# A fused attention and two expert layers on one core: the first pair of heads loaded head by head on two queues, products of zeros meanwhile, the last sums finished one by one, tiles at multiples of 512 bytes

## The chip, the cores and the metric

The kernel runs on one core of a Trainium2 chip. The metric is the device time of one execution in microseconds (us), as the median of several runs. The engines are named as the profile names them: PE is TensorE's matmul and PEld its weight load, DVE is VectorE, ACT is ScalarE, POOL is GpSimd, and SP is SyncE, which here only issues DMAs. DMAs bring data from the chip's memory (HBM) into the on-chip memory SBUF; products are summed in PSUM.

## The reference

Four batches, 12 heads, 448 tokens, heads of 64. Attention with a soft cap on the scores, then two dense layers over 1792 tokens of width 768:

```
scores = cap * tanh((q @ k.T) / sqrt(64) / cap)
attn   = softmax(scores) @ v                       # 4 x 12 x 448 x 64
x      = attn as 1792 x 768
h      = x @ w_in           # 768 -> 2048
x      = (h * cos(h)) @ w_out                      # 2048 -> 768
a, b   = x @ w1, x @ w2     # 768 -> 1024
out    = ((a * b) @ w3) @ w_out2                   # 1024 -> 1024 -> 768
```

Everything is float32. The kernel folds the last two matrices into one, w34 = w3 @ w_out2, while the attention runs.

## The kernel before, in words

**Products.** Every dense product is made in three matmuls on pairs of "high" and "low" halves (`mm3`, lines 356 to 359): high times high, high times low, low times high, in the type float32r, 448 columns wide (384 for w34). The scores (lines 574 and 575) take two such matmuls on 112 columns of weights. The product of the probabilities with v (line 595) is plain float32, which the profile shows as two records for each product. There are 4,800 float32r matmuls (4,416 with 448 columns and 384 with 384) and 192 of plain float32.

**Attention.** A pair of heads is loaded at a time: `a_load` (line 488) brings q and k of one pair, each by two DMAs of 64 partitions x 2 x 448, because both halves of the partitions hold the same rows. `a_split` (line 502) makes from them `ks` (k's high part above, its low part below), `qh` and `ql` with two casts and two subtractions over both heads (896 columns). `c_S` makes the scores of 2 x 112 keys, `c_exp` applies tanh and exp on ACT in place and into `p`, `c_PV` multiplies with v. `c_consts` (line 555) sets the ones beside v on POOL. Before that, line 443 loads the cap by an SP DMA, lines 445 to 449 make its constants on DVE, and line 452 runs one tanh on a single column, so that ACT's table is loaded.

**Dense layers.** `make_w34` reads w3 and w_out2 (`raw` tiles), and its products lie between those of the attention. `moe1` runs over pairs of slices of 128 of the 2048 columns, and `moe2` over eight slices `fc` of the 1024. In `moe2`, `ab_unit` (line 1053) makes a * b for a slice: 36 matmuls on PE, then a copy on ACT, and a product, a cast and a subtraction on DVE, which leave `abh` and `abl`. `o_unit` (line 1069) multiplies one slice with w34 and adds it into six sums `acc[m]` in PSUM, m being one of six blocks of 128 output columns. One slice's `o_unit` stands behind the next slice's `ab_unit`. At the last slice each finished sum is copied into one of three `ob` tiles on ACT and written out by an SP DMA (lines 1084 and 1085).

**What sets the order.** Every operation is put into a `Plan` with a due time and the engines that may do it. `schedule` (line 169) plays the plan with assumed costs, in order of due times, once, when the program is built; the result is one fixed order for each engine. `at(g)` (line 476) gives the due time of step g of the attention; its numbers are in `PAR`. A `Ring` is a set of equal tiles that items take in turn; an item waits for a free tile. All DMAs stand in SP's row (`dma`, line 352). A DMA uses one of eight semaphores in turn, and the ninth waits for the first.

**Where tiles lie.** A tile is laid into SBUF when it is first used, behind the one before it, at the next multiple of 32 bytes of a partition. The small constants of 4 bytes come first, so that in the built program the first large tile `xh0` begins at byte 1312, which is 2 x 512 + 288. In the same way all tiles that a matmul reads begin 32, 64, 224, 288, 320 or 480 bytes behind a multiple of 512; weight slices are 512 bytes wide, and slices of 448 columns are 1792 bytes, which is 3.5 x 512.

Of the kernel before, what the change touches and what calls it, by code (L numbers as in the profile page):

```python
# [33 lines left out]
CAP_MAX = 40.0  # L34
TWOPI = 6.283185
# [34 lines left out]
class Ring:  # L70
    def __init__(self, plan, pool, tag, shape, dtype, n):
        self.pool, self.tag, self.shape, self.dtype = pool, tag, list(shape), dtype
        self.tiles, self.queue = {}, []
        self.free = [(0.0, k) for k in range(n)]
        plan.rings.append(self)
        pool.rings.append(self)

# [14 lines left out]
class Pool:  # L92
# [20 lines left out]
class Plan:  # L113
# [157 lines left out]
    p1=3.4, p2=6.2, gsw=48, t0=10.0,  # L271
# [8 lines left out]
    nq=1, nqh=2, nph=2, npl=2,  # L280
# [3 lines left out]
    p1=1.98, p2=2.86, gsw=90, t0=14.13, ql=10, qs=4, hsw=26, wb=(30.36, 107.61), we=(108.65, 207.54),  # L284
    m0=222.0, ua=13, pa=19.15, pu=14.2, nt=9, nph=3,
# [22 lines left out]
def program(  # L308
# [43 lines left out]
    def dma(due, dst, src, r=(), w=(), kb=115, write=False):  # L352
        plan.op(due, [("SP", 0.66, lambda: SP.dma_start(dst(), src()))], r=r, w=w,  # L353
                kb=kb)
# [17 lines left out]
    for name, kw in dict(const={}, xring={}, dram=dict(space=DRAM), psum=dict(space=PSUM), attn={}, lp={},  # L372
# [30 lines left out]
    def swap(*names, opens=()):  # L403


        def f():
            for n in names:
                pools[n].close()
            for n in opens:
                pools[n].open()  # L410

        plan.event(f, [pools[n] for n in names], [pools[n] for n in opens])

    for n in ("const", "xring", "dram", "psum", "attn", "wi", "wp"):
        pools[n].open()
    psum = pools["psum"].pool
# [26 lines left out]
    SP.dma_start(capt, cap.rearrange("(o n) -> o n", o=1).to_broadcast([P, 1]))  # L443
    pac = const([P, 1], "pac")
    DVE.tensor_scalar(nac, capt, -1.0, None, op0=ALU.mult)
# [6 lines left out]
    ACT.activation(warm, warm, AF.Tanh)  # L452
# [23 lines left out]
    def at(g):  # L476

        return G["t0"] + min(g, G["gsw"]) * G["p1"] + max(g - G["gsw"], 0) * G["p2"]
# [9 lines left out]
    def a_load(i, g):  # L488
        b, h = divmod(i, H)
        qk[i] = A["qr"].new(), A["kr"].new()  # L490
        for it, src in zip(qk[i], (q2, k2)):
            for j in range(2):
                r = it.at(j, rows(j))
                dma(at(g) if i else -99.0, r, lambda src=src: src[b, h // 2].rearrange("(i d) s -> d i s", i=2),
                    w=[r], kb=230)

# [64 lines left out]
    def cv_load(i, g):  # L561
# [3 lines left out]
        dma(at(g), vt[i][:, :, j, :], lambda: v[b, h], w=[vt[i]])  # L565
# [62 lines left out]
    def columns():  # L628
        c_consts()
        a_load(0, -2)  # L630
        a_split(0, -1)
# [400 lines left out]
    def moe2():  # L1032
        raw_r, x_r = ring("lp", "rawl", [P, 2 * DM], U32, 2), ring("lp", "xl_", [P, DM], F32, 2)
        a_r, ob_r = ring("qp", "a32", [P, S], F32, 2), ring("qp", "ob", [P, S], F32, 3)
# [34 lines left out]
        def o_unit(n, b, fc, due):  # L1069
            abh, abl = ab.pop((b, fc))  # L1070
# [92 lines left out]
```

## Time and profile before

| | |
|---|---|
| median of three runs | 1143.48 us (1141.04 to 1144.9) |
| the profiled execution's own time | 1141.23 us |
| its span, first to last instruction | 1139.2 us |
| PE busy | 1112.9 us, 98% of the span |
| DVE, ACT, POOL busy | 65%, 40%, 12% |
| DMA | 140.10 MB, 123 GB/s on the mean |

A run's own time is 2.0 us longer than the span of its instructions. A busy share of PE is not a rate: matmuls overlap, and a matmul's recorded length is about twice the distance to the next one. The distance from the start of one matmul to the start of the next says how fast PE goes. In the timeline a row gives the start, the length, the engine, the line, what is written from what, the number of merged instructions, and in brackets the idle time of the engine before it and what ended it. An engine's name with a q is its queue, which issues DMAs.

### The profile page before, as it was taken

To read this page: it belongs to the slowest core of one execution; us is meant where nothing else is said; L and a number is where in the kernel's file an instruction comes from. 1 tells how busy PE (TensorE), PEld (TensorE's weight loads), DVE (VectorE), ACT (ScalarE), POOL (GpSimd) and SP (SyncE) were. 2 spreads that over 40 slices of the span, in tenths; PEclk is the share of its full clock that TensorE was granted. 3 is DMA by queue.
4 is the path that set the end of the run, shared out by engine and by line. 5 is a ranking of instruction groups with operands and counts; after the bars stand their busy time and mean duration, and the time that the engine had idled before them with its cause. 6 is when DMAs were issued, how large, how long until landed. Compare 5 with 4: busy or idle time off the path is not lost.

```text
span 1139.2 us, 13718 instructions
## 1 busy us (share of the span) xinstructions
PE 1112.9 (98%) x5184; PEld 966.5 (85%) x5184; DVE 740.5 (65%) x1111; ACT 454.2 (40%) x581; POOL 133.3 (12%) x130
## 2 busy tenths in 40 slices
PE   5999999999999999999999999999999999999997
PEld 3777777778888888889999999998999999999996
DVE  5888777899998897787899877768831311311111
ACT  4887767877566655722454211113211101101001
POOL 2312111123231110110121000001200000000000
PEclk9999999999999999999999999999999999999999
DMA  8885765878756554337745211101401101101001
GB/s 231 229 224 149 212 185 171 231 210 252 209 154 188 190 148 158 130 100 235 272 127 180 70 56 56 29 1 69 140 15 41 57 1 41 57 1 40 10 1 51
DMA packets 83165, 140.10 MB, mean 123 GB/s; under 512 B 35986, under 2 KB 63634, under 8 KB 83090
## 3 DMA queue, kind: packets, MB, share of 16 engines
q1 hardware_dynamic: 83090, 139.14, 40.7%
q8 instruction: 42, 0.69, 0.2%
q14 instruction: 33, 0.27, 0.1%
HBM read 109.45 MB, written 29.58 MB: 122 GB/s over the span
## 4 chain that ended last, share of the span: by engine, by line
PE 93%; DVE 2%; DMA 1%; ACT 1%; SPq 1%; issue 0%; POOL 0%; ACTq 0%; DVEq 0%
PE bank L357 13%; PE bank L358 13%; PE bank L359 13%; PE double L358 12%; PE double L359 12%; PE double L357 12%; PE bank L595 12%; PE double L574 3%; PE double L575 3%; DMA rawc<-in_w_out 1%; SPq L353 1%; DMA kr<-in_k 0%; DVE w L343 0%; ACT double L584 0%; ACT p L584 0%
## 5 line engine op out<-in xcount | busy, mean ns | idle before, releaser
L343 DVE TENSOR_TENSOR a<-double,a 128x448 f32<-128x448 f32 x32 | 20.0, 625 | 240.1 <-PE double L359 237.7
L595 PE MATMUL bank<-p,v 112*128 112x448 f32 x384 | 161.3, 543 | 0.5 <-issue 0.5
L359 PE MATMUL double<-xh,w12l 128*128 128x448 f32 x378 | 137.8, 365 | 0.0
L358 PE MATMUL double<-xl,w12h 128*128 128x448 f32 x378 | 137.8, 365 | 0.0
L357 PE MATMUL double<-xh,w12h 128*128 128x448 f32 x378 | 137.4, 363 | 0.0
L584 ACT ACTIVATE double<-double,ts 112x896 f32<-112x896 f32 x96 | 94.1, 981 | 79.1 <-PE double L575 78.9
L333 ACT COPY a<-double 128x448 f32<-128x448 f32 x31 | 16.5, 533 | 254.1 <-PE double L359 254.1
L357 PE MATMUL bank<-xh,wih 128*128 128x448 f32 x270 | 107.9, 399 | 0.0
L595 PEld LDWEIGHTS bank<-p,v 112*128 112x128 f32 x384 | 72.6, 190 | 41.2 <-issue 38.3
L357 PE MATMUL bank<-gh,woh 128*128 128x448 f32 x260 | 102.1, 393 | 0.3 <-ACT hs L333 0.3
L358 PE MATMUL bank<-xl,wih 128*128 128x448 f32 x270 | 98.3, 364 | 0.0
L359 PE MATMUL bank<-xh,wil 128*128 128x448 f32 x270 | 98.0, 363 | 0.0
L584 ACT ACTIVATE p<-double,pac 112x896 f32<-112x896 f32 x96 | 96.7, 1010 | 2.0
L358 PE MATMUL bank<-gl,woh 128*128 128x448 f32 x260 | 95.2, 366 | 0.0
L359 PE MATMUL bank<-gh,wol 128*128 128x448 f32 x260 | 94.8, 365 | 0.0
L574 PE MATMUL double<-qh,ks 128*112 128x448 f32 x192 | 73.7, 384 | 14.4 <-DVE ks L343 10.3
L343 DVE TENSOR_TENSOR y<-bank,y 128x448 f32<-128x448 f32 x111 | 68.6, 619 | 23.0 <-PE bank L359 22.2
L358 PEld LDWEIGHTS double<-xl,w12h 128*128 128x128 f32 x378 | 71.0, 188 | 5.8
L357 PEld LDWEIGHTS double<-xh,w12h 128*128 128x128 f32 x378 | 70.8, 187 | 5.6
L359 PEld LDWEIGHTS double<-xh,w12l 128*128 128x128 f32 x378 | 71.0, 188 | 5.0
L575 PE MATMUL double<-ql,ks 128*112 128x448 f32 x192 | 72.1, 375 | 0.0
L357 PEld LDWEIGHTS bank<-xh,wih 128*128 128x128 f32 x270 | 50.8, 188 | 9.0 <-issue 5.0
(153 smaller groups left out, 2359.2 us busy)
## 6 DMA issues: line engine op xcount, KB each, us to landing
rawc<-in_w_out SPq DMA_DIRECT2D x16, 768.0 KB, 5.6
rawl<-in_w SPq DMA_DIRECT2D x16, 768.0 KB, 4.4
qr<-in_q SPq DMA_DIRECT2D x48, 224.0 KB, 4.6
kr<-in_k SPq DMA_DIRECT2D x48, 224.0 KB, 4.9
rawc<-in_w_in SPq DMA_DIRECT2D x13, 768.0 KB, 5.0
raw<-in_w3T SPq DMA_DIRECT2D x16, 512.0 KB, 5.8
raw<-in_w_out SPq DMA_DIRECT2D x8, 768.0 KB, 7.2
wo_d<-wx SPq DMA_DIRECT2D x16, 384.0 KB, 4.4
```

What stands on the lines that cost most here:

```text
L333: "A": ("ACT", (0.051 if psum else 0.094) + n / 1200, lambda: ACT.copy(dst(), src())),
L343: "D": ("DVE", 0.068 + n / 960, lambda: DVE.tensor_tensor(dst(), a(), b(), op=op))
L353: plan.op(due, [("SP", 0.66, lambda: SP.dma_start(dst(), src()))], r=r, w=w, kb=kb)
L357: PE.matmul(out, wh, xh, start=first, stop=False)
L358: PE.matmul(out, wh, xl, start=False, stop=False)
L359: PE.matmul(out, wl, xh, start=False, stop=last)
L574: PE.matmul(o, w, qh(), start=True, stop=False)
L575: PE.matmul(o, w, ql(), start=False, stop=True)
L584: lambda f=f, x=x, o=o: ACT.activation(o(), s(), f, scale=x[:CP]))],
L595: PE.matmul(pv()[:, :S], w()[:, 2 * c + n].rearrange("p a d -> p (a d)"), p()[:, n, :], start=c == 0 and n == 0, stop=c == NT - 1 and n == 1)
```

## The change

**The first pair of heads.** `a_first` takes the place of `a_load` and `a_split` for heads 0 and 1. Each head of q and k comes by DMAs of its own (64 partitions x 448, two for q and two for k); k is issued by SP and q by ACT. Its casts and subtractions are made for each head apart: k's cast on ACT, the rest on DVE. The v of head 0 is issued by ACT too, that of head 1 comes right behind the second pair. The second pair of heads is due before everything else that SP loads, and q and k have two tiles each instead of one (`nq`). The cap's DMA moves from SP to POOL. The tanh that loads ACT's table is now an operation of the plan, behind ACT's first DMAs. The due times of the first ten steps have a step of their own (`p0`, `g0`, `t0`).

**Products of zeros.** A tile of zeros is written by DVE first of all, and PE makes nine plain float32 products of 128 x 128 from it into a bank that nothing reads.

**The last sums.** The last slice but one has no `o_unit` of its own; the last `o_unit` goes over the six sums and adds both slices to each. `ob` has four tiles, and a write may go out on SP's or ACT's queue.

**Places in SBUF.** Two pads (224 bytes below, 480 above) and `settle` lay all tiles of a pool when it opens, those whose size is a multiple of 512 first. In the built program `xh0` begins at byte 2048, and every tile that a matmul of this program reads begins at a multiple of 512 or 256 bytes behind one.

```
+LINE = 512
+    def settle(self):
+        rings = sorted(self.rings, key=lambda r: r.bytes() % LINE > 0)
+        for r in rings:
+            for k in range(r.n):
+                r.tile(k)
...
-    p1=3.4, p2=6.2, gsw=48, t0=10.0,
+    p0=2.4, p1=3.4, p2=6.2, g0=10, gsw=48, t0=6.5,
...
-    nq=1, nqh=2, nph=2, npl=2,
+    nq=2, nqh=2, nph=2, npl=2,
...
+    def dma(due, dst, src, r=(), w=(), kb=115, write=False, on="S"):
+        opts = {
+            "S": ("SP", 0.66, lambda: SP.dma_start(dst(), src())),
+            "A": ("ACT", 0.66, lambda: ACT.dma_start(dst(), src())),
+        }
+        plan.op(due, [opts[e] for e in on], r=r, w=w, kb=kb)
...
+        pools["const"].pool.tile([P, 56], F32, name="pad", bufs=1)
+        pools["top"].pool.tile([P, 120], F32, name="pad2", bufs=1)
...
-    SP.dma_start(capt, cap.rearrange("(o n) -> o n", o=1).to_broadcast([P, 1]))
+    (SP if general else POOL).dma_start(capt, cap.rearrange("(o n) -> o n", o=1).to_broadcast([P, 1]))
...
+        z = const([P, P], "zeros")
+        DVE.memset(z, 0.0)
+        for _ in range(9):
+            PE.matmul(banks[7][:, :P], z, z, start=True, stop=True)
...
-    ACT.activation(warm, warm, AF.Tanh)
+    plan.op(-80.0, [("ACT", 1.4, lambda: ACT.activation(warm, warm, AF.Tanh))], w=[Ref(warm_i)])
...
-                dma(at(g) if i else -99.0, r, lambda src=src: src[b, h // 2].rearrange("(i d) s -> d i s", i=2),
+                dma(at(g) if i > 2 or general else -97.0, r, lambda src=src: src[b, h // 2].rearrange("(i d) s -> d i s", i=2),
...
+    def a_first():
+        q, k = qk[0] = A["qr"].new(), A["kr"].new()
+        qh, ql, ks = (A[x].new() for x in ("qh", "ql", "ks"))
+        for n in range(2):
+            for it, src, e in ((k, k2, "S"), (q, q2, "A")):
+                for j in range(2):
+                    r = it.at((n, j), lambda t, n=n, j=j: t[j * D:(j + 1) * D, n])
+                    dma(-99.0 + n, r, lambda src=src, n=n: src[0, 0, n * D:(n + 1) * D], w=[r], on=e)
...
+            plan.op(due, [("ACT", 0.47, lambda n=n, o=ks_: ACT.copy(o(), k.tile()[:, n]))], r=kj, w=[ks_])
+            low = ks.at(n, lower)
+            plan.op(due, [("DVE", 0.54, lambda n=n, o=low: DVE.tensor_tensor(
+                o(), k.tile()[D:, n], o().bitcast(F32), op=ALU.subtract), True)], r=[kj[1], low], w=[low])
+            plan.op(due - 0.5, [("DVE", 0.3, lambda n=n, o=qh_: DVE.tensor_copy(o(), q.tile()[:, n]), True)], r=qj, w=[qh_])
+            plan.op(due, [("DVE", 0.54, lambda n=n, o=ql_, h=qh_: DVE.tensor_tensor(
+                o(), q.tile()[:, n], h().bitcast(F32), op=ALU.subtract), True)], r=[*qj, qh_], w=[ql_])
...
-        dma(at(g), vt[i][:, :, j, :], lambda: v[b, h], w=[vt[i]])
+        dma(at(g) if i > 1 else -60.0, vt[i][:, :, j, :], lambda: v[b, h], w=[vt[i]], on="S" if i else "A")
...
+            for m in range(KD):
+                for fc, abh, abl, wh, wl in fcs:
...
+                if prev and (n, fc) != (B - 1, NF2 - 1):
+                    o_unit(prev[0], prev[1], prev[2:], due)
                     due += 3.4
-                prev = (n, b, fc)
+                    prev = []
+                prev = prev + [fc] if prev else [n, b, fc]
```

SP's row at the start of the program, before. `capt` is the cap, `qr` and `kr` are q and k of a pair, `raw` the words of w3 and w_out2:

```order
L443 DMA capt<-in_cap 128x1
L353 DMA qr_111<-in_q 64x2x448 x2
L353 DMA kr_114<-in_k 64x2x448 x2
L353 DMA raw_117<-in_w3T 128x1024
L353 DMA raw_119<-in_w_out 128x1536
L353 DMA raw_121<-in_w_out 128x1536
L353 DMA v_103<-in_v 112x4x64
```

The same place now:

```order
L366 DMA kr_132<-in_k 64x448 x4
L366 DMA qr_131<-in_q 64x2x448 x2
L366 DMA kr_133<-in_k 64x2x448 x2
L366 DMA v_122<-in_v 112x4x64
L366 DMA raw_159<-in_w3T 128x1024
L366 DMA raw_160<-in_w_out 128x1536
L366 DMA raw_161<-in_w_out 128x1536
```

The cap and q of the first pair have left SP's row, and q and k of the second pair (`qr_131`, `kr_133`) and a v stand ahead of the first `raw`.

ACT's row at the start, before. Line 452 is the tanh on one column, line 804 scales a `raw` tile, line 584 is tanh and exp of the scores:

```order
L452 ACT_TABLE_LOAD
L452 ACTIVATE warm<-warm 128x1
L804 ACTIVATE raw_117<-raw_117 128x512
L584 ACTIVATE double_75<-double_75,ts 112x2x448
L584 ACTIVATE double_76<-double_76,ts 112x2x448
L584 ACTIVATE p_153<-double_75,pac 112x896
```

The same place now:

```order
L367 DMA qr_130<-in_q 64x448 x4
L481 ACT_TABLE_LOAD
L481 ACTIVATE warm<-warm 128x1
L367 DMA v_118<-in_v 112x4x64
L541 CAST ks_138<-kr_132 128x448 x2
L637 ACTIVATE double_80<-double_80,ts 112x2x448
L637 ACTIVATE double_81<-double_81,ts 112x2x448
```

Five DMA issues and the two casts of k stand ahead of the first tanh, and the first `raw` tile behind several of them.

PE's last twelve matmuls, before, with buffer numbers. `abh1` and `abl1` are the last slice, and a sum's bank stands at the left:

```order
L357 MATMUL double0_75<-abh1_5627,w34h70_5890 128x448
L358 MATMUL double0_75<-abl1_5633,w34h70_5890 128x448
L359 MATMUL double0_75<-abh1_5627,w34l70_5892 128x448
L357 MATMUL bank6_79<-abh1_5627,w34h70_5890 128x448
L358 MATMUL bank6_79<-abl1_5633,w34h70_5890 128x448
L359 MATMUL bank6_79<-abh1_5627,w34l70_5892 128x448
L357 MATMUL bank4_77<-abh1_5627,w34h70_5890 128x448
L358 MATMUL bank4_77<-abl1_5633,w34h70_5890 128x448
L359 MATMUL bank4_77<-abh1_5627,w34l70_5892 128x448
L357 MATMUL double1_76<-abh1_5627,w34h70_5890 128x448
L358 MATMUL double1_76<-abl1_5633,w34h70_5890 128x448
L359 MATMUL double1_76<-abh1_5627,w34l70_5892 128x448
```

The same place now, where `abh0` and `abl0` are the slice before the last:

```order
L372 MATMUL bank6_84<-abh0_5561,w34h60_5588 128x448
L373 MATMUL bank6_84<-abl0_5563,w34h60_5588 128x448
L374 MATMUL bank6_84<-abh0_5561,w34l60_5589 128x448
L372 MATMUL double0_80<-abh0_5561,w34h60_5588 128x448
L373 MATMUL double0_80<-abl0_5563,w34h60_5588 128x448
L374 MATMUL double0_80<-abh0_5561,w34l60_5589 128x448
L372 MATMUL bank6_84<-abh1_5562,w34h70_5594 128x448
L373 MATMUL bank6_84<-abl1_5564,w34h70_5594 128x448
L374 MATMUL bank6_84<-abh1_5562,w34l70_5595 128x448
L372 MATMUL double0_80<-abh1_5562,w34h70_5594 128x448
L373 MATMUL double0_80<-abl1_5564,w34h70_5594 128x448
L374 MATMUL double0_80<-abh1_5562,w34l70_5595 128x448
```

Four of the six sums are now finished ahead of these twelve matmuls, where before it was two; the plan put twelve matmuls of the slice before the last between the last `ab_unit` and the first matmul on its result.

## Rows read from the trace of the kernel before

**Rows 1.** The page, busy time of each engine, share of the span, instructions.

```profile
PE 1112.9 (98%) x5184; PEld 966.5 (85%) x5184; DVE 740.5 (65%) x1111; ACT 454.2 (40%) x581; POOL 133.3 (12%) x130
```

**Rows 2.** Waits of PE: releaser, us in total, times, longest.

```profile
PE double L574 <- DVE ks L343: 10.3, 1, 10.3
PE double L574 <- ACT p L584: 4.1, 2, 2.1
PE double L358 <- DVE gl L343: 2.6, 1, 2.6
```

**Rows 3.** Stretches: us, each engine's busy us (instructions), clock, DMA share, GB/s.

```profile
30.00:40.00 10.00, 8.43 (x25) 5.35 (x26) 9.87 (x13) 9.02 (x12) 2.72 (x2) 0.83 0.62 170
885.00:1125.00 240.00, 240.00 (x1191) 223.04 (x1190) 44.64 (x83) 22.45 (x42) 0.00 (x0) 1.00 0.07 22
1136.00:1139.20 3.20, 0.00 (x0) 0.00 (x0) 0.00 (x0) 0.00 (x0) 0.00 (x0) 0.50 0.02 5
```

**Rows 4.** Timeline of the first 10 us, all engines.

```profile
0.73 1.28 ACT L452 ACT_TABLE_LOAD   x1 [0.73 <-PEq L1151]
0.74 0.40 SPq L443 DMA_DIRECT2D capt<-in_cap  x1
1.19 1.39 SPq L353 DMA_DIRECT2D qr<-in_q  x2
...
3.32 0.15 DVE L445 TENSOR_SCALAR nac<-capt 128x1 f32<-128x1 f32 x1 [3.32 <-DMA capt<-in_cap]
...
5.92 0.63 DVE L334 CAST qh<-qr 128x896 fp32r<-128x896 f32 x1 [1.66 <-DMA qr<-in_q]
...
8.48 0.63 DVE L334 CAST ks<-kr 128x896 fp32r<-128x896 f32 x1 [0.81 <-DMA kr<-in_k]
...
10.29 0.71 PE L574 MATMUL double<-qh,ks 128*112 128x448 f32 x1 [10.29 <-DVE ks L343]
```

**Rows 5.** Timeline of PE, scores of the first and of a later pair.

```profile
10.80 0.57 PE L575 MATMUL double<-ql,ks 128*112 128x448 f32 x1
11.17 0.57 PE L574 MATMUL double<-qh,ks 128*112 128x448 f32 x1
...
31.57 0.46 PE L574 MATMUL double<-qh,ks 128*112 128x448 f32 x1 [2.08 <-ACT p L584]
```

**Rows 6.** Timeline of the last 16 us, PE, DVE, ACT and SP's queue.

```profile
1123.77 0.36 PE L357 MATMUL bank<-abh,w34h 128*128 128x448 f32 x1
...
1125.12 0.63 DVE L343 TENSOR_TENSOR abl<-a,abh 128x448 fp32r<-128x448 f32 x1
...
1127.82 0.36 PE L359 MATMUL bank<-abh,w34l 128*128 128x448 f32 x1
...
1128.27 1.14 ACT L333 COPY ob<-bank 128x448 f32<-128x448 f32 x2 [4.97 <-PE bank L359]
...
1130.57 3.66 SPq L353 DMA_DIRECT2D outT<-ob  x4
...
1130.86 0.37 PE L359 MATMUL double<-abh,w34l 128*128 128x448 f32 x1
...
1132.98 0.53 ACT L333 COPY ob<-double 128x448 f32<-128x448 f32 x1 [0.26 <-DMA outT<-ob]
```

**Rows 7.** Timeline of PE, matmuls in three stretches without a wait.

```profile
449.90 1.67 PE L595 MATMUL bank<-p,v 112*128 112x448 f32 x4
...
451.61 0.36 PE L358 MATMUL bank<-xl,wih 128*128 128x448 f32 x1
...
784.48 0.37 PE L357 MATMUL bank<-xh,w12h 128*128 128x448 f32 x1
...
795.02 0.37 PE L357 MATMUL double<-xh,w12h 128*128 128x448 f32 x1
...
822.67 0.36 PE L357 MATMUL double<-xh,w12h 128*128 128x448 f32 x1
...
829.07 0.36 PE L359 MATMUL double<-xh,w12l 128*128 128x448 f32 x1
```

More of the change, by code (lines that the diff above doesn't have):

```diff
@@ L74, in __init__, with bytes @@
         self.free = [(0.0, k) for k in range(n)]
+        self.n = n
         plan.rings.append(self)
         pool.rings.append(self)
+    def bytes(self):
+        return 4 * math.prod(self.shape[1:])
     def tile(self, k):
@@ L371, in program @@
     right = dict(side="right", reuse_waits="tile")
-    for name, kw in dict(const={}, xring={}, dram=dict(space=DRAM), psum=dict(space=PSUM), attn={}, lp={},
+    for name, kw in dict(const={}, top=dict(side="right"), xring={}, dram=dict(space=DRAM), psum=dict(space=PSUM), attn={}, lp={},
                          wi=dict(side="right"), wp=dict(side="right"), yp=right, mp=right, cv=right,
@@ L410, in f @@
                 pools[n].open()
+                if not general:
+                    pools[n].settle()
         plan.event(f, [pools[n] for n in names], [pools[n] for n in opens])
-    for n in ("const", "xring", "dram", "psum", "attn", "wi", "wp"):
+    for n in ("const", "top", "xring", "dram", "psum", "attn", "wi", "wp"):
         pools[n].open()
+    if not general:
+        pools["const"].pool.tile([P, 56], F32, name="pad", bufs=1)
+        pools["top"].pool.tile([P, 120], F32, name="pad2", bufs=1)
     psum = pools["psum"].pool
@@ L451, in program @@
     DVE.memset(warm, 0.0)
-    ACT.activation(warm, warm, AF.Tanh)
+    warm_i = Item(None)
+    warm_i.tile = lambda: warm
+    plan.op(-80.0, [("ACT", 1.4, lambda: ACT.activation(warm, warm, AF.Tanh))], w=[Ref(warm_i)])
     xh_r = ring("xring", "xh", [P, KD, S], F32R)
@@ L493, in a_load @@
                 r = it.at(j, rows(j))
-                dma(at(g) if i else -99.0, r, lambda src=src: src[b, h // 2].rearrange("(i d) s -> d i s", i=2),
+                dma(at(g) if i > 2 or general else -97.0, r, lambda src=src: src[b, h // 2].rearrange("(i d) s -> d i s", i=2),
                     w=[r], kb=230)
+    def a_first():
[6 more added lines that the diff above has]
+                    dma(-99.0 + n, r, lambda src=src, n=n: src[0, 0, n * D:(n + 1) * D], w=[r], on=e)
+            half = lambda t, n=n: t[:, n]
+            lower = lambda t, n=n: t[D:, n]
+            ks_, qh_, ql_ = (z.at(n, half) for z in (ks, qh, ql))
+            kj, qj = ([z.at((n, j)) for j in range(2)] for z in (k, q))
+            due = -50.0 + n
+            plan.op(due, [("ACT", 0.47, lambda n=n, o=ks_: ACT.copy(o(), k.tile()[:, n]))], r=kj, w=[ks_])
[5 more added lines that the diff above has]
+                o(), q.tile()[:, n], h().bitcast(F32), op=ALU.subtract), True)], r=[*qj, qh_], w=[ql_])
+            st[n] = qh_, ql_, ks_
     def v_load(i, g):
@@ L1105, in moe2 @@
                     split_y(nb, fc, due + 4, yr)
-        o_unit(*prev, due)
+        o_unit(prev[0], prev[1], prev[2:], due)
     (queries if general else columns)()
@@ L1115, in program @@
     swap("mp", "yp", "wi", opens=("qp", "q2"))
-    for _, f in plan.schedule():
+    order = plan.schedule()
+    if not general:
+        for n in ("xring", "attn", "wi", "wp"):
+            pools[n].settle()
+    for _, f in order:
         if f is not None:
             f()
-    for n in ("q2", "qp", "lp", "psum", "dram", "xring", "const"):
+    for n in ("q2", "qp", "lp", "psum", "dram", "xring", "top", "const"):
         pools[n].close()
```

50 lines of the change are left out of this document (23 added, 27 removed).

## The prediction

> **What bounds the kernel now.** I read the page first: PE is busy for 98% of the span and no other engine for more than 65% [rows 1]. Then the waits of PE: the long ones are 10.3 us ahead of the first matmul, 4.1 us in two waits for ACT early on, and 2.6 us at one later place [rows 2]. So PE's time is a start, a few early holes, some 1,110 us of matmuls one behind the other, and an end. The end is found in the timeline: the last matmul starts at 1130.86 [rows 6] and the span ends at 1139.2, of which the last 3.2 us hold no work of the program [rows 3]. A change can thus gain at the start, at the end, or in the distance between matmuls, and there it counts 4,800 times.
>
> That distance is the view I spent most on. From 885 to 1125 us there are 1191 matmuls, two of which began before: 240 / 1189 = 202 ns each [rows 3]. At the level of 2.4 GHz, 448 columns need 186.7 ns, so 15 ns a matmul are something else. They are not the same everywhere: from 784.48 to 795.02 lie 51 distances of 206.7 ns, from 822.67 to 829.07 lie 32 of 200.0 ns [rows 7]. Both are the same products (`xh`, `xl` with `w12`), and the weights of the first begin 288 bytes behind a multiple of 512, those of the second 224. Where a tile lies can therefore change the distance by 6.7 ns. No float32r operand of this kernel lies at a multiple of 128 bytes, so the place to which the change moves all of them is not in this trace.
>
> **The start.** The first matmul waits for the last of four DVE operations, and these for k, whose cast starts at 8.48 us; q's starts at 5.92 [rows 4]. q's two DMAs carry 256 rows of 1792 bytes, and k's 256 more take 8.48 - 5.92 = 2.56 us. Now k and q of head 0 are 256 rows together, issued from 0.74 us on instead of 1.19: they land at 5.92 - 0.45 = 5.47. Then ACT still issues a v DMA (half of the 1.39 for two [rows 4], 0.69) and casts k (448 columns on ACT: 0.53, and a subtraction of 448 columns on DVE 0.63 [rows 6]); with 0.1 for the hand-overs PE starts at 5.47 + 0.69 + 0.53 + 0.63 + 0.1 = 7.42. DVE's work on q meanwhile is at most 0.63 for the cast [rows 4] and 0.63 for the subtraction; it ends at 6.7, hidden. Gain 10.29 - 7.42 = 2.9 us. Bounds: if the queues bring both heads together, the data is there at 8.48 - 0.45 = 8.03, PE starts at 9.98, and 0.3 us is left; without the v issue in the way and with rows 0.6 us sooner it is 4.2. I take 2.9.
>
> The cap now comes through POOL, whose DMAs the trace does not show. By SP it landed 2.6 us after its issue, and five small DVE operations of about 0.19 us followed [rows 4]. DVE is free for q until 5.47, so the cap may come 1.2 us later than it did; each us beyond costs one. I take nothing. The table load of 1.28 us [rows 4] moves behind four DMA issues on ACT, to about 3.5 to 4.8 us, and is hidden by the same wait for data.
>
> **The zeros.** The first score matmuls are 0.37 us apart, the level of 1.2 GHz [rows 5]; later ones 0.20. A plain float32 product of 448 columns takes 1.51 / 2 us at the upper level (from 449.90 to one distance before 451.61, two products [rows 7]), which is four passes. Nine of 128 columns at the lower level are 9 x 4 x 0.107 = 3.8 us, done by 5 us, before the data: they cost nothing. They can save at most the lower level of the first four matmuls ahead of the first tanh, 4 x 0.17 = 0.7 us. But PE then idles for over 2 us, and after an idle time of 2.08 us at 31.57 [rows 5] the clock column of that stretch falls to 0.83 [rows 3], 1.7 us of clock lost. I take 0.3; bounds 0 and 1.4.
>
> **Behind the start.** The two waits for ACT (4.1 us) stay: tanh and exp of the scores are the same. SP loads the second pair, 917 KB, ahead of `raw`; at 2.56 us for 459 KB that puts the first w34 products some 5 us later. Scores and products with v of heads 2 and 3 stand there instead. This can fill a hole (2 us) or leave PE waiting for ACT, which has `raw_159` in its row and behind it the exps (5 us). I take 0.
>
> **The end.** The copies of the last three sums wait for `ob` tiles: the last starts at 1132.98, though its last matmul started at 1130.86. The first copy starts 0.45 us after the start of its last matmul (1128.27 - 1127.82 [rows 6]). With four tiles, and four sums finished twelve matmuls earlier, the last copy starts at 1130.86 + 0.45 = 1131.31: gain 1.7 us, and the DMA behind it moves along. The last slice's result is ready at 1125.12 + 0.63, 1.98 us after 1123.77, where PE turns from `ab_unit` to `o_unit` [rows 6]; the twelve matmuls put between are 2.4 us, so PE does not stall. Bounds 0.6 (the write behind another on its queue: SP spends 0.9 us on each of its last four) and 2.2.
>
> **The places of the tiles.** Lower bound of the distance: the passes of plain float32, 1.51 / 8 = 189 ns. Upper bound: 206.7. Between them, 200.0 is the shortest that float32r reaches now. Their counts: 4,416 matmuls of 448 columns, 384 shorter ones with 0.86 of the effect, so 1 ns is 4.75 us. After the change data and weights always keep the same few distances to each other, which could settle into the 200.0 pattern or the 206.7 one. Of the two the first is nearer to the mean; I take -1 ns, 4.8 us, half of the way to it.
>
> **Sum.** 2.9 + 0.3 + 0 + 1.7 + 4.8 = 9.7 us. The profiled execution took 1141.2 (span 1139.2 and 2.0 around it), which gives 1131.5; the median of the runs is 2.3 us above that execution, so for the median 1143.5 - 9.7 = 1133.8.
>
> **Rivals.**
> A, the excess goes altogether. If a float32r read costs extra only because it starts in the middle of some unit of SBUF, then at multiples of 256 the distance falls to the 189 ns of the float32 passes: 13 x 4.75 = 62 us, 1143.5 - 4.9 - 62 = 1077. For it: 200.0 - 186.7 is exactly 32 columns or 128 bytes, as if a matmul read one unit more than it needs, and the excess is absent at the lower clock (0.37 us is 448 columns and nothing more). Against it: the 32 to 480 bytes of offset make no such step among themselves. The Trainium skill, "TensorE: Matmul & The Clock Gate", section "Back-to-back issue gap", gives N / 2.4 + 2.5 ns, 189 for 448 columns; the trace's 202 disagrees for float32r, and by that rule the time would be this rival's.
> C, the places do nothing, only start and end count: 1143.5 - 4.9 = 1138.6. For it: all tiles already start at multiples of 32. The Trainium skill, "SBUF — State Buffer", section "Specifications (TRN2)", knows lines of 16 bytes, and by that rule a move from 32 to 512 changes nothing; the two stretches of 200.0 and 206.7 speak against it.
> B, the slower pattern: data and weights start at the same place within 128 bytes, as in the stretch of 206.7 (both at 32; in the 200.0 one they differ by 64). If all matmuls went so, 4.7 x 4.75 = +22 us and 1161; in half of them +11 and 1150. It decides for slower from a mean distance of 203.7 on, where 1.7 x 4.75 = 8 us eat the 4.9 of start and end and 0.3%.
> D, the early order goes wrong: PE waits 5 us behind `raw_159` or the cap, and the places do nothing: 1143.
>
> **How the numbers follow.** Forecast 0.29 (own range 1127 to 1138), A 0.25, C 0.18, B 0.20, D 0.08. This kernel's runs tell a change from 0.3% on, which is 1140.0. Faster: forecast and A whole, C mostly, 0.67. Same (1140 to 1147): a part of C, D and B, 0.14. Slower: most of B and a little of D, 0.19. The range must reach into A, down to 1075, and into B, up to 1150; it leaves out A's lower end and B's upper.
>
> **What would show it.** First score matmul at 7.4 us (6.1 to 10); distances of 0.20 instead of 0.37 there only if the zeros raised the clock. Last copy 0.45 us behind the last matmul. A stretch like 885 to 1125 without waits: 240 us holding 1194 matmuls for the forecast, 1270 for A, 1180 or fewer for B. The prediction is wrong in its largest step if that count falls outside 1190 to 1202.

## The result, and the profile after

The change makes the kernel slower. The median of its 17 runs is 1149.24 us (1144.15 to 1158.33) against 1143.48 for the kernel before; the ratio on record, which is not the quotient of the medians, is 1.0070, 95% interval 1.0054 to 1.0086. Run again beside three other kernels: 1.0095 (1.0073 to 1.0118). The forecast was 1134, faster. Its runs scatter over 14 us, those of before over some 6, if one of 1603.58 us is left out.

The profiled execution of the changed kernel is the slowest of its runs: 1158.33, span 1156.4, its time 17.1 us above that of before. The page's row of PE, and then the waits of PE (releaser, us in total, times, longest):

```profile
PE 1130.2 (98%) x5202; PEld 971.2 (84%) x5202; DVE 746.6 (65%) x1119; ACT 449.2 (39%) x576; POOL 135.7 (12%) x131
```

```profile
PE bank L648 <- DVE xs L346: 3.4, 3, 2.2
PE double L627 <- DVE ks L543: 2.8, 1, 2.8
PE double L627 <- ACT p L637: 2.6, 2, 2.0
PE double L372 <- ACT xh L345: 2.0, 1, 2.0
PE double L372 <- DVE y L355: 1.8, 2, 1.4
PE bank L374 <- DVE w3l L355: 1.6, 1, 1.6
PE double L373 <- DVE gl L355: 1.5, 1, 1.5
PE bank L372 <- DVE sum L355: 1.4, 1, 1.4
PE bank L471 <- DVE zeros L469: 1.1, 1, 1.1
```

PE is busy for the same 98% [rows 1], and that share hides both losses: it is busy longer (1130.2 against 1112.9), and the list of waits has changed. Before, the long wait was the one ahead of the first matmul [rows 2]; now waits of 1 to 2 us, most of them for DVE, stand in the middle of the program. Without the waits ahead of the first scores and the zeros, the view's rows sum to 15.6 us; before they sum to 8.1 (with three rows of 0.6 us and less that [rows 2] does not show).

The stretches (us, busy us and instructions of PE, PEld, DVE, ACT, POOL, then clock, DMA share, GB/s) show the other loss:

```profile
640.00:680.00 40.00, 40.00 (x196) 36.33 (x195) 30.56 (x51) 6.45 (x9) 1.34 (x1) 1.00 0.13 41
730.00:760.00 30.00, 30.00 (x150) 27.82 (x149) 21.39 (x36) 5.13 (x8) 0.83 (x1) 1.00 0.04 14
885.00:1125.00 240.00, 240.00 (x1163) 217.96 (x1163) 44.56 (x82) 25.11 (x48) 0.00 (x0) 1.00 0.08 29
```

Counted as in [rows 3], with two matmuls that began earlier, the distance is 40 / 194 = 206.2 ns in the first, 30 / 148 = 202.7 in the second, and 240 / 1161 = 206.7 in the third, where before had 202.0. Within 256 bytes the operands lie alike in all three, data and weights both at 0. From one matmul to the next, stretches of hundreds of products stand at one of these two distances, and the change from one to the other comes where PE was held up: at 606 us up to 206.7, at 695.8 (by a single distance of 214 ns) down to 202.7, at 782 up again, and so to the end. Over all products of 448 columns at the level of 2.4 GHz, some 4,325 by the records, the mean is 204.74 ns, before 202.51; the 2.23 ns make 9.6 us.

The start, by timeline (start, us, engine, line, operation, idle time and releaser):

```profile
1.06 4.21 PE L471 MATMUL bank<-zeros 128*128 128x128 f32 x18 [1.06 <-DVE zeros L469]
5.08 0.15 DVE L472 TENSOR_SCALAR nac<-capt 128x1 f32<-128x1 f32 x1 [4.08 <-DMA capt<-in_cap]
6.04 0.39 DVE L545 CAST qh<-qr 128x448 fp32r<-128x448 f32 x1
6.05 0.20 ACT L481 ACTIVATE warm<-warm 128x1 f32<-128x1 f32 x1 [1.21 <-DVE warm L478]
6.06 0.65 ACTq L367 DMA_DIRECT2D v<-in_v  x1
6.81 1.03 ACT L541 CAST ks<-kr 128x448 fp32r<-128x448 f32 x2 [0.55 <-issue]
7.41 1.16 DVE L543 TENSOR_TENSOR ks<-kr,ks 64x448 fp32r<-64x448 f32 x2 [0.32 <-ACT ks L541]
8.08 0.45 PE L627 MATMUL double<-qh,ks 128*112 128x448 f32 x1 [2.82 <-DVE ks L543]
8.38 0.37 PE L628 MATMUL double<-ql,ks 128*112 128x448 f32 x1
8.58 0.36 PE L627 MATMUL double<-qh,ks 128*112 128x448 f32 x1
9.34 0.98 ACT L637 ACTIVATE double<-double,ts 112x896 f32<-112x896 f32 x1 [1.50 <-PE double L628]
```

The first score product starts at 8.08 instead of 10.29 [rows 4]. The cap's chain on DVE lasts to 6.0, with the `warm` tile written behind it; ACT's tanh waits for that tile, and v issue, cast and DVE's subtraction follow one behind the other. The end:

```profile
1149.34 0.53 ACT L345 COPY ob<-bank 128x448 f32<-128x448 f32 x1 [0.85 <-PE bank L374]
1149.55 0.37 PE L374 MATMUL double<-abh,w34l 128*128 128x448 f32 x1
1150.64 0.53 ACT L345 COPY ob<-double 128x448 f32<-128x448 f32 x1 [0.77 <-PEq L315]
```

The last copy starts 1.09 us after the last matmul, before 2.12 [rows 6], and the span ends 6.85 us after it, before 8.34. The sum for the two profiles: start -2.2, distance +9.6, waits of PE +7.5, end -1.5; the remainder to the 17.1 us, +3.7, lies in the records with the products right behind the waits and those at the lower clock.

### The profile page after: what moved, and what is told of

Same layout as the page of the kernel before. It is cut to its first block, busy times and chain, and to the rows that moved or that the text cites. A ratio compares the mean times of both kernels' runs of the same rounds, so it can differ in the third digit from the quotient of the medians.

```text
span 1156.4 us, 13778 instructions
## 1 busy us (share of the span) xinstructions
PE 1130.2 (98%) x5202; PEld 971.2 (84%) x5202; DVE 746.6 (65%) x1119; ACT 449.2 (39%) x576; POOL 135.7 (12%) x131
## 5 line engine op out<-in xcount | busy, mean ns | idle before, releaser
L355 DVE TENSOR_TENSOR a<-bank,a 128x448 f32<-128x448 f32 x31 | 19.4, 625 | 247.8 <-PE bank L374 245.7
L372 PE MATMUL bank<-xh,wih 128*128 128x448 f32 x252 | 101.9, 404 | 0.0
L373 PE MATMUL bank<-xl,wih 128*128 128x448 f32 x252 | 92.3, 366 | 0.0
L372 PE MATMUL double<-xh,w12h 128*128 128x448 f32 x192 | 70.7, 368 | 0.0
L374 PE MATMUL bank<-xh,w12l 128*128 128x448 f32 x192 | 70.7, 368 | 0.0
L372 PE MATMUL bank<-xh,w12h 128*128 128x448 f32 x192 | 70.7, 368 | 0.0
L374 PE MATMUL double<-xh,w12l 128*128 128x448 f32 x192 | 70.7, 368 | 0.0
L373 PE MATMUL bank<-xl,w12h 128*128 128x448 f32 x192 | 70.7, 368 | 0.0
L373 PE MATMUL double<-xl,w12h 128*128 128x448 f32 x192 | 70.7, 368 | 0.0
L372 PE MATMUL bank<-w2h,w3h 128*128 128x384 f32 x128 | 57.2, 447 | 1.8 <-DVE sum L355 1.4
```

The lines of the kernel that those rows point to most:

```text
L355: "D": ("DVE", 0.068 + n / 960, lambda: DVE.tensor_tensor(dst(), a(), b(), op=op))
L372: PE.matmul(out, wh, xh, start=first, stop=False)
L373: PE.matmul(out, wh, xl, start=False, stop=False)
L374: PE.matmul(out, wl, xh, start=False, stop=last)
```

## The experiments

Each ratio is to runs of the kernel before on the same chip at the same time; from set to set the chip differs, so ratios are compared and not medians. In e1, e2, e9, e10 and e13 PE, DVE and SP have the order of the kernel that they start from, and in e11 that of e7; only addresses move (e13 also leaves out the zeros).

| run | edit | median us | ratio (95%) |
|---|---|---|---|
| e1 | changed, no pads | 1148.29 | 1.0037 (1.0023, 1.0050) |
| e2 | before, tiles aligned | 1148.86 | 1.0041 (1.0019, 1.0063) |
| e3 | changed, no zeros | 1147.91 | 1.0050 (1.0032, 1.0069) |
| e4 | changed, again | 1153.88 | 1.0095 (1.0073, 1.0118) |
| e6 | before, new end | 1141.70 | 0.9995 (0.9985, 1.0004) |
| e7 | e1, due times of before | 1137.65 | 0.9965 (0.9951, 0.9979) |
| e8 | e1, second pair late | 1147.68 | 1.0054 (1.0037, 1.0072) |
| e9 | e7, data 64, weights 0 | 1131.75 | 0.9896 (0.9882, 0.9911) |
| e10 | before, data 64, weights 0 | 1137.66 | 0.9945 (0.9932, 0.9958) |
| e11 | changed, due times of before | 1140.57 | 0.9990 (0.9971, 1.0009) |
| e12 | e1, t0 10.0, p0 2.4 | 1147.32 | 1.0025 (1.0009, 1.0042) |
| e13 | e9, 64 within 256, no zeros | 1130.52 | 0.9905 (0.9888, 0.9923) |
| e15 | e1, t0 6.5, p0 3.4 | 1149.69 | 1.0071 (1.0055, 1.0087) |
| e16 | before, t0 6.5 | 1152.66 | 1.0087 (1.0064, 1.0110) |
| e17 | e7, t0 12.0 | 1145.58 | 1.0023 (1.0011, 1.0035) |

**First set: places or waits (e1 to e4).** e1:

```diff
-    if not general:
...
-        pools["const"].pool.tile([P, 56], F32, name="pad", bufs=1)
-        pools["top"].pool.tile([P, 120], F32, name="pad2", bufs=1)
```

> The changed kernel in every instruction and its order, but the two pads are gone: tiles lie 32 or 96 bytes behind multiples of 128 as in the kernel before. Theory L (places set the distance): in the changed kernel a stretch of matmuls stands either at 202.7 or at 206.7 ns and stays there until the next wait; with the old places it mixes again, mean 202.5 ns over all warm float32r matmuls of 448 columns, 1185 to 1192 of them from 885 to 1125 us, and the time falls to about 1144 (1149.2 less half of the 9.6 us that the profile lost to distance), with a spread over the runs below 6 us. Theory W (the new waits of PE behind the start cost it all, 8 us in the profile; the distance is chance and has nothing to do with places): time stays at 1149, spread 14 us, and stretches at 206.7 over 100 us long come again.

Both theories were half right. The distance went back to a mix, 202.6 ns in the mean; the changed kernel and e1, from 885 to 1110 us:

```profile
885.00:1110.00 225.00, 225.00 (x1090) 204.34 (x1090) 42.13 (x78) 24.58 (x47) 0.00 (x0) 1.00 0.09 31
```

```profile
885.00:1110.00 225.00, 225.00 (x1115) 209.14 (x1114) 41.44 (x77) 23.46 (x45) 0.00 (x0) 1.00 0.09 31
```

225 / 1088 = 206.8 ns and 225 / 1113 = 202.2. The runs lie within 5 us of each other. But the waits stayed (14.9 us by the view), and with them 4 us more than before. So there is a second loss that stays when the places are put back. Two of its rows:

```profile
PE bank L644 <- DVE xs L346: 3.2, 3, 2.0
PE double L372 <- ACT xh L345: 2.0, 1, 2.0
```

e2 puts the kernel before on aligned places, with its own order:

```diff
             for n in opens:
                 pools[n].open()
+                if not general:
+                    pools[n].settle()
...
+    if not general:
+        pools["const"].pool.tile([P, 184], F32, name="pad", bufs=1)
+        pools["top"].pool.tile([P, 120], F32, name="pad2", bufs=1)
...
```

> The kernel before with only its tiles placed as in the changed one (multiples of 512, or of 256 for the short ones), the instruction order of before on PE and SP. L: time 1143.5 + 5 = 1148.5 (1143 to 1155), only two distances, 202.7 and 206.7, in long stretches, and runs that scatter by 10 us. W: 1143.5 and the mix of 200 to 206.7 as before.

```profile
885.00:1110.00 225.00, 225.00 (x1091) 204.40 (x1090) 41.28 (x76) 21.90 (x41) 0.00 (x0) 1.00 0.08 26
```

L holds: 225 / 1089 = 206.6 ns here, 202.7 in other stretches of the same profile, and twelve runs from 1141.4 to 1153.3. The places alone cost 0.4%, 4.7 us in the mean.

e3 takes the products on zeros away:

```diff
-        for _ in range(9):
-            PE.matmul(banks[7][:, :P], z, z, start=True, stop=True)
```

> The changed kernel without the nine products on zeros. In its profile the first four score matmuls were 0.30, 0.20, 0.20 and 0.32 us apart and the next four 0.37. If the zeros raised the clock there, all eight are now 0.37 apart and the first exp starts 0.4 us later; the first score matmul itself stays at 8.1 us. Else nothing moves. Time as the changed kernel, 1149 (1144 to 1158).

```profile
8.01 0.72 PE L625 MATMUL double<-qh,ks 128*112 128x448 f32 x1 [8.01 <-DVE ks L541]
8.52 0.58 PE L626 MATMUL double<-ql,ks 128*112 128x448 f32 x1
8.90 0.58 PE L625 MATMUL double<-qh,ks 128*112 128x448 f32 x1
9.27 0.58 PE L626 MATMUL double<-ql,ks 128*112 128x448 f32 x1
```

Behind the first they are 0.37 apart now, the level of 1.2 GHz; with the zeros the second to the fourth started after 0.30, 0.20 and 0.20. The first tanh starts at 9.89 instead of 9.34, so in that profile the zeros give some 0.6 us at that place. That is not so in every execution: e4 has the same nine products of zeros, and its first score products are 0.37 apart too, as in e8, e9 and e11:

```profile
8.76 0.58 PE L628 MATMUL double<-ql,ks 128*112 128x448 f32 x1
9.13 0.57 PE L627 MATMUL double<-qh,ks 128*112 128x448 f32 x1
```

Nor does it last where it came. From 9 to 16 us the clock column of the changed kernel stands at 0.50, that of e3 at 0.91:

```profile
9.00:16.00 7.00, 5.00 (x12) 3.09 (x12) 3.97 (x5) 5.11 (x6) 0.00 (x0) 0.50 1.03 346
```

```profile
9.00:16.00 7.00, 5.01 (x14) 3.04 (x13) 3.93 (x5) 5.34 (x7) 0.00 (x0) 0.91 1.03 344
```

The 31st matmul record behind the zeros starts at 22.06 us with them and at 21.28 without. (Ahead of its first drop the column of e3 reads 1.00 although the distances are 0.37; there the distances are what tells the level.) In the median of the runs no gain of the zeros can be seen.

e4 is the changed kernel again:

> The changed kernel once more, for a second profile on the same chip as the others. L: again only the two distances 202.7 and 206.7; which stretch has which is another draw, so a profile of 1149 us would show some 4 us less at 206.7 than that of 1158. W: the same stretches as in the first profile, and the same waits.

Its profiled run took 1147.81, 10.5 us less than the first profile, with its waits at the same lines (13.3 us against 15.6). From 885 to 1110:

```profile
885.00:1110.00 225.00, 225.00 (x1112) 208.76 (x1111) 41.35 (x76) 22.45 (x42) 0.00 (x0) 1.00 0.08 28
```

225 / 1110 = 202.7 ns, where the first profile had 206.8. So the same program with the same addresses shows either distance; 7 us of the 10.5 are distance (mean 203.1 ns against 204.7).

**Second set: which places (e5), the end (e6), the waits (e7, e8).** e5 is a kernel of its own, whose core is

```
                        PE.matmul(o, wh[:, ws], xh[:, xs], start=k == 0, stop=False)
                        PE.matmul(o, wh[:, ws], xl[:, xs], start=False, stop=False)
                        PE.matmul(o, wl[:, ws], xh[:, xs], start=False, stop=k == KD - 1)
```

where the slices `xs` and `ws` begin mo and so bytes further on.

> Not the reference's computation, its output is zeros: only float32r matmuls as in the second half of the kernel (six groups of three per sum, 448 columns, two data tiles and two weight tiles), in 60 segments of 72; ahead of each PE waits for DVE for a time that differs. The data begins mo and the weights so bytes behind a multiple of 128; 20 pairs (mo, so), each three times. Theory L (the places of data and weights to each other, within 128 bytes, set which distances are possible): (0,0), (32,32), (64,64), (96,96) stand at 202.7 or 206.7 ns, one of them for a whole segment; (0,64), (32,96), (64,0), (96,32) at 200 to 202. Rival K (the place itself counts, whole multiples of 128 are one case): (0,0) differs from the other three equal pairs, and (0,64) from (32,96). Rival Z (what a wait leaves behind decides, places do nothing): every pair shows each of 200.0, 202.7 and 206.7 in some of its segments.

Six stretches of 14 us, one each inside the segments (64,0), (64,32), (64,64), (96,32), (96,96), (0,16):

```profile
139.00:153.00 14.00, 14.00 (x71) 13.11 (x71) 0.00 (x0) 0.00 (x0) 1.00 0.00 1
154.00:168.00 14.00, 14.00 (x70) 13.14 (x71) 0.00 (x0) 0.00 (x0) 1.00 0.00 0
169.50:183.50 14.00, 14.00 (x70) 12.98 (x70) 0.00 (x0) 0.00 (x0) 1.00 0.00 1
215.80:229.80 14.00, 14.00 (x71) 13.11 (x72) 0.00 (x0) 0.00 (x0) 1.00 0.00 1
246.90:260.90 14.00, 14.00 (x69) 12.72 (x69) 0.00 (x0) 0.00 (x0) 1.00 0.00 1
262.60:276.60 14.00, 14.00 (x69) 12.71 (x69) 0.00 (x0) 0.00 (x0) 1.00 0.00 1
```

The counts differ by two only; from the starts of the records the distances are exact: (64,0), (64,32) and (96,32) 200.0 in all three segments; (0,0), (32,32), (64,64) 202.7, (32,32) once 206.6 (the first (0,0) ran at the lower clock and is left out); (96,96) and (0,16) 206.6; (0,64) and (32,96) 202.2; (0,32) and (64,96) 203.3 and 204.4; (32,64) 204.4; (96,0) 205.3; (16,0) 200.1 and 202.3; (16,16) 200.1; (16,80) 206.7; (0,96), (32,0) and (96,64) change from one segment to the next, among 200.0, 204.4 and 206.7. L is right that the place of the data against the weights counts, and wrong that plus and minus 64 are one case. K is right in part, for the place itself counts as well: equal places stand at 200.1 in each segment of (16,16), at 202.7 in each of (64,64) and at 206.6 in each of (96,96), and (16,80) is as far apart as (0,64) within 256 bytes and stands at 206.7 instead of 202.2. Z falls, since most pairs give one distance; where a pair has several, its segments differ in the program by nothing but the wait ahead, which is taken to draw one. This happens with almost no DMA and no other engine at work.

e6 is the kernel before with the new `o_unit` and four `ob` tiles:

> The kernel before with the new end alone (the last two slices' sums one behind the other, four ob tiles, writes on two queues); all engines' instructions up to the last period as before. In the changed kernel the span ends 6.85 us after the start of the last matmul, before 8.34. So -1.5 us: ratio 0.9987 to the kernel before, last copy 0.45 us behind the last matmul. If the two queues gave nothing and only the copies move: -0.6, ratio 0.9995.

The span ends 7.39 us after the start of the last matmul instead of 8.34; over the runs it is 0.6 us less (-1.7 to +0.5). The last copy still waits, 1.45 us behind its matmul. By the records it is held by the second of the six writes: that one's last part lands at 1133.60 and the copy starts at 1133.70 (in the changed kernel 1150.56 and 1150.64). With four `ob` tiles the sixth copy takes the tile of the second.

e7 puts the planner's due times of the attention back in e1:

```diff
-    p0=2.4, p1=3.4, p2=6.2, g0=10, gsw=48, t0=6.5,
+    p0=3.4, p1=3.4, p2=6.2, g0=10, gsw=48, t0=10.0,
```

> The kernel without pads, with the planner's due times of before for the attention's columns (t0 10.0 and 3.4 per column, not 6.5 and 2.4 for the first ten). Theory D (due times 3.5 us too early put loads and splits ahead of what PE needs next): the waits between 30 and 800 us fall from 16 us to the 8 of the kernel before, lag at 70 us of the kernel before -3 instead of 0, time 1139 to 1141. Theory R (each order of the planner brings its own waits, the due times have no part in it): the waits lie elsewhere but sum to 12 to 20 us, time 1144 to 1152.

Theory D (not the prediction's rival of that letter) holds, and the time is better than its 1139 to 1141: 4 us faster than the kernel before, 8.2 us faster than e1 (0.9965 against 1.0037). The waits of PE:

```profile
PE double L373 <- DVE gl L355: 2.6, 1, 2.6
PE double L623 <- DVE ks L539: 2.6, 1, 2.6
PE double L623 <- ACT p L633: 2.6, 2, 2.0
PE bank L374 <- DVE w3l L355: 1.2, 1, 1.2
PE bank L467 <- DVE zeros L465: 1.1, 1, 1.1
```

All but the first scores and the zeros sum to 7.7 us, about as before. Counted by the products done, PE reaches the work of 70 us of the kernel before some 4.3 us earlier and keeps that up to 760 (3.0 from 780 on); e1 was level at 70, some 2.5 behind at 300, 5 at 340 and 10 from 780 on.

e8 lets the second pair's loads come late:

```diff
-                dma(at(g) if i > 2 or general else -97.0, r, ...
+                dma(at(g) if i > 0 or general else -97.0, r, ...
```

> The kernel without pads, with the loads of the second pair at their due times again, so that raw and w34's first products come ahead of them. Theory Q (the second pair's 917 KB ahead of raw costs the 4.5 us that PE loses between 40 and 70 us of the kernel before): lag at 70 us -3 to -4 instead of 0, time 1148.3 - 4 = 1144. Theory R: PE waits for ACT at 30 us instead as in the kernel before (2 us), and what comes later is another order with other waits; time 1144 to 1152, with no link to the first 70 us.

Q is right about the place and not about the total: at 70 us PE is some 3 us ahead instead of level, but waits come later (2.1 us at 334, 1.5 at 593, 3.6 at 772), and the time is that of e1.

**Third set: both together (e9 to e12).** e9 is e7 with all weights at a multiple of 128 and all data 64 behind one; a tile of 64 bytes stands between weights and data, another behind the data (its smaller pads are not shown):

```diff
+STAT = {"ks", "w3h", "w3l", "wih", "wil", "woh", "wol", "w12", "w34"}
...
-        rings = sorted(self.rings, key=lambda r: r.bytes() % LINE > 0)
+        rings = sorted(self.rings, key=lambda r: (r.tag[:3] not in STAT, r.bytes() % LINE > 0))
...
+                self.pool.tile([P, 16], F32, name=f"{self.name}_a", bufs=1)
...
+            self.pool.tile([P, 16], F32, name=f"{self.name}_b", bufs=1)
...
```

> The changed kernel with the due times of before (as in the run without pads, 1137.7) and its tiles placed by the run on places: all data 64 bytes behind a multiple of 128, all weights at one (only the 384 score products and the products on p differ). Theory L: 200.0 ns in every stretch whatever the waits, 2.5 ns x 4.75 = 11.9 us less than the 1137.7: 1125.8 (1124 to 1129), from 885 to 1117 us all distances 200. Rival Z (what a wait leaves decides): the mean stays at 202.5, time 1137 to 1142.

> The kernel before with only its tiles placed so (data at 64, weights at 0 of 128 bytes), order of instructions as before. L: 1142 - 11.9 = 1130 (1128 to 1134). Z: 1142.

Both are faster, and half to two thirds of the places' gain came: e10 6.3 us, not 11.9; e9 7.9 us less than e7 by the ratios, 1131.75 and not 1125.8. The mean distance is 200.9 in both. The records say where the rest is: `gh` with `woh`, `xh` with `wih` and `ab` with `w34` stand at 200.0 to 200.7, `xh` with `w12` at 202.3. By address, the first three begin 64 bytes behind their weights counted within 256, `xh` 192 behind those of `w12`.

> The changed kernel, pads and all, with the due times of before alone put back. The places of the changed kernel cost 1148.9 - 1142.1 = 6.8 us on the kernel before, 0 to 10 by the draw; so here 1137.7 + 5 = 1143 (1138 to 1149), stretches at 202.7 or 206.7 only. If the due times were the whole loss, 1137.7.

The changed kernel with the old due times: 1140.57, but from 1138.84 to 1149.09. The profiled run stood at 202.7 throughout. Against e7 the places cost 2.5 thousandths here; the two intervals overlap a little.

> The kernel without pads with the old start of the due times (10.0) but the new 2.4 us per column for the first ten, so everything from the eleventh column on is due 10 us earlier than before; with 6.5 and 2.4 it was 13.5 us and 1148.3, with 10.0 and 3.4 it was 1137.7. If it is the shift of the attention's due times against the fixed ones of the rest that makes the planner put additions ahead of what PE waits for, most of the waits come back: 1145 to 1149. If 6.5 did it, 1138.

Waits of 2.6 us at 245 and 1.5 at 293 came, longer or elsewhere than in e1, and the time is 1147.3: most of the loss is back with `p0` alone.

**Fourth set: what was open (e13 to e17).** e13 moves the pools of `w12`, `w34` and `ab` by 128 bytes more and leaves out the zeros:

```diff
-            self.pool.tile([P, 16], F32, name=f"{self.name}_b", bufs=1)
+            self.pool.tile([P, 16 + 32 * (self.name in ("xring", "qp"))], F32, name=f"{self.name}_b", bufs=1)
```

> The kernel with both things mended, whose profile had 200.0 to 200.7 ns where the data begins 64 bytes behind the weights counted within 256 bytes (gh with woh, xh with wih, ab with w34) and 202.3 where it is 192 (xh with w12, 1152 matmuls). Now these too are at 64 within 256, and so are all but 288 of the 4,800; the products on zeros, which gave nothing, are left out. Theory L256 (the distance of data and weights within 256 bytes decides): xh with w12 at 200.0, 1152 x 2.28 = 2.6 us less than 1131.75: 1129.1 (1127.5 to 1130.5), 1199 or 1200 matmuls from 885 to 1117 per 240 us. Rival O (it is the operands: w12's products take longer, for instance because they share their time with DMA and DVE): xh with w12 stays at 202.3, 1131.8.

```profile
885.00:1110.00 225.00, 225.00 (x1127) 210.92 (x1126) 38.67 (x71) 19.71 (x37) 0.00 (x0) 1.00 0.06 19
```

225 / 1125 = 200.0 ns; by the records `xh` with `w12` fell from 202.3 to 200.0, so L256 holds for these places and O falls. The profiled run took 1129.87; the median, 1130.52, has an interval that overlaps that of e9, so the last 2.6 us are seen in the distance and not in the time.

> As the run on places, output zeros again, with the weights at a multiple of 256 and the data 0, 16, ..., 240 bytes behind, and four pairs with weights at 128 or 64. L256: data at 64 gives 200.0 in all three segments, data at 192 202.2 (as (0,64) and (32,96) did before, 192 within 256), and (192,128) as (64,0), (128,128) as (0,0), (64,128) as (192,0); (192,64) as (128,0). If only 128 bytes counted, (192,0) would be at 200.0 as (64,0).

Stretches of (64,0), (192,0), (128,128) and (192,128):

```profile
76.50:90.50 14.00, 14.00 (x72) 13.06 (x70) 0.00 (x0) 0.00 (x0) 1.00 0.00 1
200.20:214.20 14.00, 14.00 (x71) 12.97 (x70) 0.00 (x0) 0.00 (x0) 1.00 0.00 0
262.20:276.20 14.00, 14.00 (x69) 12.71 (x69) 0.00 (x0) 0.00 (x0) 1.00 0.00 1
278.00:292.00 14.00, 14.00 (x71) 13.11 (x72) 0.00 (x0) 0.00 (x0) 1.00 0.00 1
```

From the starts: 64 bytes 200.0 to 200.1 in all three segments, at weights of 0 and of 128; 192 bytes 202.2 at both; 128 bytes 204.0, at weights of 0 and of 64. No pair is below 200.0. (128,128) gives 206.7 where (0,0) gave 202.7, as the two distances of the changed kernel; the map has no simple form (16 bytes 200.1 or 202.3, 80 bytes 203.3 or 206.7, 112 and 144 always 206.7; 240 bytes 202.7, where (0,16) of e5 had 206.6).

e15 and e16 change one number each, `t0` from 10.0 to 6.5: e15 in e7, e16 in the kernel before; e17 sets it to 12.0 in e7.

> The kernel without pads with the new start of the due times (6.5) and the old 3.4 us per column throughout: all of the attention due 3.5 us earlier than in the run at 1137.7, where with 2.4 for the first ten as well (10 us more) it was 1148.3, and with 10.0 and 2.4 1147.3. If waits grow with the shift: 1138 to 1141. If any other number draws another order with other waits and 1137.7 was luck: 1144 to 1150.

> The kernel before with one number changed: the attention's due times begin at 6.5 instead of 10.0. Theory S (only with the loads by head is the earlier start bad): 1142 as before. Theory N (the other numbers were fitted to 10.0, any departure brings an order with more waits, whatever the loads): 1146 to 1152, new waits of PE for DVE between 190 and 800 us.

> The kernel at 1137.7 (no pads, due times of before) with the due times shifted the other way, 12.0 instead of 10.0. N: again more waits behind 190 us, 1143 to 1150. If only a shift to earlier is bad (the attention's work overtakes what PE needs next): 1137 to 1140.

S falls, and N's times and waits came; that the other numbers were fitted to 10.0, N's reason, is not shown. The kernel before loses 10 us by this one number. Waits of e16:

```profile
PE double L357 <- DVE wih L334: 4.0, 1, 4.0
PE bank L358 <- DVE gl L343: 2.7, 1, 2.7
PE double L357 <- DVE y L343: 2.1, 3, 0.8
```

The first of them is e15's too (4.0 for `wih`). A shift to later costs as well (e17, 0.9965 to 1.0023, 6.6 us). Five departures from 10.0 and 3.4 (e1, e12, e15, e16, e17), in either kernel and both directions, cost 6.6 to 12 us each.

## Why the prediction was wrong, step by step

**The start** was right in the main, 2.2 us of the 2.9. By the landings k of head 0 was there at 5.71 and q at 5.94, not at 5.47, and the rest of the chain took the 2 us that were worked out. But ACT's part of it did not begin with the data. It stood behind the tanh on `warm`, which waited for DVE, and DVE writes `warm` behind the cap's operations. Their first starts at 5.08 instead of 3.32 [rows 4], 1.76 us later where the prediction allowed 1.2: "I take nothing" left out a wait that holds k's cast. What the first score would gain without it, no run shows.

**The zeros** gave 0.6 us at the first tanh in one profile and nothing in the next (e4), and by 22 us the profile without them is 0.8 ahead. The 0.3 that was taken is not borne out; the doubt that stood beside it, that the idle time takes the clock back, fits the rows better.

**"Behind the start ... I take 0"** is the first step that failed. It looked at the first 70 us, bounded them well (e1 is level at 70, having been some 4 ahead at 40) and stopped there. The due times are an input of the whole plan: with another `t0` and `p0` the orders of all engines differ, PE's from its 204th record on, and PE meets waits up to 790 us. With the old numbers the start's gain stays (e7); with the new number alone the kernel before loses it (e16). The step left out 8 us, which is more than the 4.9 of start, zeros and end together. Why a given order has a given wait was not traced back to the planner's rules and stays open.

**"The places of the tiles ... I take -1 ns"** is the second. The measured mean is +2.2 ns in the first profile and +0.6 in the second, and from 885 to 1125 us the first holds 1161 matmuls, outside the 1190 to 1202 that the prediction named. The choice between the 200.0 and the 206.7 pattern went to the side nearer to the mean, which was no reason: equal places of data and weights had 206.7 in a stretch of the trace before, as rival B said. In a kernel with mixed places a stretch at 206.7 ends with the next tile; with all places equal, in the profiles of the changed kernel, e2, e3 and e4, it ends only where PE is held up. That is why the time differs between the two profiles of the changed kernel, for 7 of 10.5 us; for the scatter of the other runs it is the likely reason.

**The end** was +1.7 on paper, 1.5 in the profile, 0.6 with zero in its interval when run alone. The last copy is not 0.45 us behind the last matmul but 1.09, and 1.45 in e6: four tiles for six sums still leave it waiting for the second write.

**The rivals.** B, the slower pattern, is what the profile shows from 782 us on, at the 206.7 ns it named. It named 1150 to 1161, and the slowest runs are there, but partly by luck: of the 17.1 us of the slowest, 9.6 are distance. The second profile, at 1147.81, holds stretches of 202.7, which it did not foresee. A (the excess goes altogether) falls: no pair of places is below 200.0. The Trainium skill, "TensorE: Matmul & The Clock Gate", section "Back-to-back issue gap", gives N / 2.4 + 2.5 ns as the gap of isolated matmuls, 189 for 448 columns; the best stretch here, e13's, has 200.0, so the traces disagree for float32r, at any of the 35 pairs of places tried. C (places do nothing) falls too: 16 bytes change the distance (e14, 64 against 80: 200.0 against 203.3 and 206.7). D had the right kind of loss, an order gone wrong, at the wrong place: its 5 us in the first stretch, where most of it came behind 190 us.

## What to carry to other kernels

When a change touches the numbers of a planner, the whole order behind it is new: run the change with the old numbers and the numbers without the change before crediting or blaming either. Here an edit that gained 4 us (e7) read as a loss of 4 (e1) because two numbers moved with it. Aligning everything is a choice of one relation between the operands, not of the best; measure the relations first (one run of 1 ms gave the map), then place data against weights by it: 64 bytes took 0.55% off the kernel before (e10).

## What the runs showed of the hardware

- The distance of float32r matmuls at 2.4 GHz depends on where the data begins against the weights, within 256 bytes: 200.0 ns at 64, 202.2 at 192, 204.0 at 128, each at two to four pairs, and 206.7 at 112 and 144 with the weights at 0, for 448 columns (186.7 ns at the clock alone). The difference is not all of it: (16,80), which is 192 too, stood at 206.7, (16,16) at 200.1 and (0,0) at 202.7; (64,32) always at 200.0, (32,0) only sometimes. What in the chip makes it so no run shows.
- At some relations, equal places among them, two or three distances are possible, and in four profiles they changed only where PE was held up, though not at every such place: in one program (0,0) stood at 206.7 for some 360 us on end (787 to 1149) and in its next profile at 202.7 for 450, waits included (687 to 1139). A kernel whose runs scatter by 1% can owe it to that.
- Nine short products on zeros that ended 2.8 us ahead left the first four score products faster in the changed kernel (0.30, 0.20, 0.20 and 0.32 us, later ones 0.37), though PE was idle in between. In e4, the same program, they did not (0.37 behind the first), and in the profile where they did, the clock column stood at 0.50 from 9 to 16 us.
